# Rounding and absolute value of the first two chunks' angles on VectorE, clearing of the AT tiles on GpSimd, and another list of the order, in a gated linear attention with a low-rank mixer

## The chip, the cores and the metric

The kernel runs on one core of a Trainium2 chip. A core has five engines that each work through their own stream of instructions in order: TensorE (PE in the profile, with PEld for its loads of weights), VectorE (DVE), ScalarE (ACT), GpSimd (POOL) and SyncE (SP), which here only issues DMA transfers. They wait for one another by semaphores. The metric is the time of one execution on the device, in microseconds (us), and the number compared is the median of the runs.

## The reference, cut to what matters

Inputs are float32 for the attention (B = 4 batches, H = 8 heads, S = 768 tokens, D = 48 values a head); the weights of the mixer come in float64.

```python
mag = sqrt(a_re**2 + a_im**2)
scale = minimum(mag, 0.999) / (mag + 1e-6)
ar, ai = a_re * scale, a_im * scale          # a complex gate for each token, head and value
for t in range(S):                           # a complex state of 48 x 48 for each head
    S_re, S_im = ar*S_re - ai*S_im + k v^T, ar*S_im + ai*S_re
    y[t] = q S_re
x = y as (B, S, 384)
u = x + (x^T @ U @ V)^T                      # U: 768 x 32, V: 32 x 768, over the tokens
out = u + maximum(u @ w_ch1, 0) @ w_ch2      # 384 -> 1536 -> 384
```

The loop over tokens isn't run as such. Each batch is cut into chunks of 128 tokens. Within a chunk the product of the gates up to a token is exp(sum of log magnitudes) times a rotation by the sum of angles. So the queries and keys are scaled by exp(±sum) and by cosine and sine of the summed angle, and one matrix product gives all pairs of tokens. Sums over the tokens are matmuls with a triangular matrix of ones ("prefix"). A state of 96 x 48 for each head goes from chunk to chunk.

## The kernel before, in words

**Work.** There are 24 chunks i of 128 tokens (i = 0 to 23, six in a batch), taken in pairs, the groups g = 0 to 11. For group 0 each of its two chunks is treated by itself from the first step on; later groups are treated as pairs. The functions are:

- `magnitudes_of` and `ratio_of` (L674 to L731): squares, logarithms and exponentials on ACT and the sums between them on DVE give the logarithm of the clipped magnitude. The check of the smallest sums stands at L689, the first combination of squares at L686 (chunks of group 0), L715 begins the same for later groups, and L723 and L726 are its later sums.
- `within(i)`: L751 is PE's prefix sum into a bank of PSUM, and L754 are two Exps on ACT, with both signs, into `es`.
- `totals`: the last row of `es` goes out to DRAM (L762) and comes back spread over partitions as T (L765); L767 keeps its minimum on DVE.
- `turns_of` and `angles(i)` (L774 to L821): arctangent on ACT, then the prefix sum of the angles on PE (L811, and L814 by its caller, in whole turns; L817 carries in the last row of the chunk before). L819, on ACT, writes MAGIC − angle into F, which rounds to a whole number; L820, on DVE, takes MAGIC off again and adds the angle, so that F is the part of a turn that is left.
- `waves_of(i)` (L828 to L839): the absolute value of F (ACT, L837), the sine of F (L838) and the cosine, as a sine of the absolute value (L839), into `cs`.
- `prep(i)`: DVE multiplies queries and keys by `es` and by `cs` (L857 and L861, both by the helper `mul` in L462) into QKC; PE turns them (L872 to L874); ACT copies them from the banks into QK (L878).
- `chain(i)`: products of queries and keys (L901), their allowed part copied into an AT tile (L904), the state's product (L921 to L924), the state G after the first half chunk (GM, L932 or by a helper in L468) and after the second, times T (L462), and the outputs xo.
- `mixer(m)` from L976: the products with U, V, w_ch1 and w_ch2, which are most of PE's time. `single` (L587 to L618) makes float32 weights of float64 ones in integer steps, on DVE for the first six pieces.

Many lines of the profile are those of helpers: L459 is every ACT activation, L462 every DVE product, L465 every DVE sum, L468 a bounded sum.

**Buffers.** There are six banks of PSUM that most PE results share in turn, three QKC tiles, two AT tiles, and two F, `es` and `cs` buffers. The two AT tiles are cleared once, at L553 to L555, since L904 writes only the allowed places.

**Order.** Nothing runs while the functions are called: each registers operations by `PE(...)`, `ACT(...)`, `DVE(...)`, `POOL(...)` and `SP(...)`, with an engine, a cost, a rank and the data that it reads and writes, and each gets a number (2207 in all). Then the operations are issued in the order of a list, `ORDER`, written out by hand as numbers. What stands on one engine runs in the list's order; between engines only the data count. Two more things belong to the list: `SPARE` sets idle matmuls ahead of some operations (2 ahead of 122, 10 ahead of 132, 14 ahead of 193 and 5 ahead of 217), and `WARM` registers 7 and 5 more of them as operations 2205 and 2206. Their numbers are fixed; they are issued whether PE waits or not.

The operations that the change touches by number: 106 and 107 are the last two ACT steps (logarithm and Exp) that make x of chunk 0; 110 and 111 are chunk 0's two Exps of L754, 123 and 124 those of chunk 1; 122 is chunk 1's L751 pass, and 130 the load of ACT's next table. 133 and 138 are L819 for chunks 0 and 1, 134 and 139 their L820, 140 and 143 their L837, 141 and 144 their L838, and 142 and 145 their L839. 10 and 13 are steps of a weight piece on DVE, 191 is chunk 0's product of queries and keys with `es`, 192 and 196 are its two QKC products, and 151 is L715 of the next group.

Of the kernel before, what the change touches and what calls it, by code (L numbers as in the profile page):

```python
# [318 lines left out]
def kernel(  # L319
# [49 lines left out]
    RATIO, TINY = 1, 2.0 ** -60  # L369

    WARM = (7, 5)
    AT_ONCE = (0, 1, 2)
    WP = 768

    fast = ExitStack()
# [45 lines left out]
    def c_act(n):  # L421
        return 0.22 + 0.0008 * n
# [1285 lines left out]
```

## Time and profile before

| what | value |
|---|---|
| median of 3 runs | 535.88 us (535.63 to 535.94) |
| the profiled execution | 535.69 us |
| its span, first to last instruction | 533.9 us |
| mean granted TensorE clock | 0.998 |
| PE busy | 514.2 us, 96% of the span, 7494 instructions |
| DVE busy | 438.2 us, 82%, 863 instructions |
| ACT busy | 295.8 us, 55%, 531 instructions |
| POOL busy | 30.5 us, 6%, 58 instructions |
| read from memory and written | 33.60 MB and 4.76 MB |

The profile is one execution of the program as the hardware profiler saw it. Its times begin at the first instruction. In a row of a timeline the first number is the start, the second the duration (of all the instructions of the row, where it says x2 or more), then come engine, line, operation, the tiles out<-in, partitions x elements, and in brackets how long the engine was idle just before and what ended it. In a row of the waits the numbers are us in total, times, and the longest. Busy PE counts matmuls whose ends are modelled; register, branch and semaphore instructions aren't counted as busy.

### The profile page before, as it was taken

The numbers are of one execution on the slowest core, as the hardware profiler recorded it, in microseconds if no ns is written. First come the engines' busy times: TensorE is split into PE (matmuls) and PEld (weight loads), VectorE is DVE, ScalarE is ACT, GpSimd is POOL, SyncE is SP. The second block draws the span as 40 slices with busy tenths as digits, with TensorE's granted clock in tenths as the row PEclk, the third lists the DMA queues.
The fourth block names the chain that finished last, engine by engine and source line by source line (L and its number), as shares of the span: only waits on it lengthen the run. The fifth ranks groups of instructions, "written<-read, shape, count | busy, mean of one in ns | idle before, by whom it ended". The sixth has DMA issues, their size and how long they took to land.

```text
span 533.9 us, 17164 instructions
## 1 busy us (share of the span) xinstructions
PE 514.2 (96%) x7494; PEld 468.1 (88%) x7494; DVE 438.2 (82%) x863; ACT 295.8 (55%) x531; POOL 30.5 (6%) x58
## 2 busy tenths in 40 slices
PE   2899999999999999999999999999999999999996
PEld 1777786757989989999999999999999999999996
DVE  7898988999999998897886887786878866877842
ACT  5889998893776866546647655543555412221000
POOL 1000000001020001001100001100010000000010
PEclk9999999999999999999999999999999999999999
DMA  9967985565233423601534150500240000000002
GB/s 226 206 114 194 191 145 163 171 107 112 41 75 92 63 46 80 111 1 29 118 53 83 33 106 25 98 9 23 47 70 26 2 2 1 1 2 1 1 28 97
DMA packets 150706, 39.95 MB, mean 75 GB/s; under 512 B 145880, under 2 KB 147440, under 8 KB 150624
## 3 DMA queue, kind: packets, MB, share of 16 engines
q1 hardware_dynamic: 148544, 34.63, 32.3%
q0 software_dynamic: 2080, 4.15, 2.3%
q8 instruction: 61, 1.00, 0.8%
q14 instruction: 21, 0.17, 0.1%
HBM read 33.60 MB, written 4.76 MB: 72 GB/s over the span
## 4 chain that ended last, share of the span: by engine, by line
PE 81%; DVE 11%; ACT 3%; issue 2%; DMA 2%; SPq 0%; DVEq 0%; ACTq 0%
PE down L1313 20%; PE few L1181 13%; PE bank L1181 12%; PE bank L1484 7%; PE bank L872 4%; PE bank L901 4%; PE up L1074 3%; PE bank L959 3%; PE bank L921 3%; PE bank L951 2%; DVE QKC L462 2%; PE bank L1036 1%; PE bank L747 1%; PE bank L751 1%; PE bank L811 1%
## 5 line engine op out<-in xcount | busy, mean ns | idle before, releaser
L878 ACT COPY QK<-bank 112x512 f32<-112x512 f32 x96 | 51.8, 591 | 18.2 <-PE bank L872 17.9
L1313 PE MATMUL down<-w,h 128*128 128x192 f32 x288 | 53.6, 331 | 0.0
L462 DVE TENSOR_TENSOR QKC<-qk,cs 128x768 f32<-128x768 f32 x48 | 45.0, 951 | 4.9 <-ACT cs L459 4.7
L459 ACT ACTIVATE gate<-gate 128x768 f32<-128x768 f32 (+1 forms) x50 | 39.8, 798 | 16.3 <-DVE wide L719 12.7
L1313 PEld LDWEIGHTS down<-w,h 128*128 128x128 f32 x288 | 47.0, 190 | 0.9
L465 DVE TENSOR_TENSOR xo<-bank,xo 128x192 f32<-128x192 f32 x78 | 25.3, 350 | 24.9 <-PE bank L1484 16.0
L1189 ACT COPY h<-few 128x512 f32<-128x512 f32 x35 | 20.3, 585 | 30.0 <-PE few L1181 29.9
L1074 PE MATMUL up<-uT,w 128*128 128x256 f32 x144 | 34.0, 385 | 0.2
L456 ACT ACT_TABLE_LOAD x24 | 30.8, 1283 | 1.1 <-PEq L1692 0.7
L1074 PEld LDWEIGHTS up<-uT,w 128*128 128x128 f32 x144 | 26.6, 190 | 5.0 <-DVE xo L465 0.5
L1181 PE MATMUL bank<-extra,w 128*128 128x128 f32 x232 | 30.3, 276 | 0.0
L872 PE MATMUL bank<-ident,QKC 64*112 64x64 f32 x768 | 29.1, 221 | 1.0 <-DVE G L468 0.4
L872 PEld LDWEIGHTS bank<-ident,QKC 64*112 64x112 f32 x768 | 24.4, 130 | 6.2 <-DVE QKC L462 1.4
L459 ACT ACTIVATE es<-bank 128x384 f32<-128x384 f32 x48 | 20.3, 495 | 16.6 <-PE bank L747 15.8
L797 POOL DMA_DIRECT2D gate<-F x15 | 12.5, 832 | 285.2 <-DVE F L820 167.2
L1181 PEld LDWEIGHTS bank<-extra,w 128*128 128x128 f32 x232 | 28.3, 192 | 0.1
L1313 PE MATMUL down<-stage 128*128 128x192 f32 x144 | 28.0, 332 | 0.2 <-DVE xo L465 0.2
L465 DVE TENSOR_TENSOR xo<-down,xo 128x192 f32<-128x192 f32 (+1 forms) x58 | 22.0, 386 | 7.1 <-PE down L1313 6.9
L901 PE MATMUL bank<-QK 112*64 112x64 f32 x768 | 26.6, 224 | 0.0
L901 PEld LDWEIGHTS bank<-QK 112*64 112x64 f32 x768 | 24.2, 138 | 1.3 <-issue 0.5
L459 ACT ACTIVATE cs<-F 128x384 f32<-128x384 f32 x48 | 23.3, 516 | 3.0 <-DVE F L820 2.9
L1313 PEld LDWEIGHTS down<-stage 128*128 128x128 f32 x144 | 23.5, 190 | 1.2 <-DVE xo L465 0.5
(249 smaller groups left out, 1228.6 us busy)
## 6 DMA issues: line engine op xcount, KB each, us to landing
stage<-in_moe_w_ch_dram SPq DMA_DIRECT2D x12, 768.0 KB
gate<-in_a_re_dram SPq DMA_DIRECT2D x24, 192.0 KB
gate<-in_a_im_dram SPq DMA_DIRECT2D x24, 192.0 KB
qk<-in_q_dram SPq DMA_DIRECT2D x24, 192.0 KB
qk<-in_k_dram SPq DMA_DIRECT2D x24, 192.0 KB
VP<-in_v_dram SPq DMA_DIRECT2D x24, 192.0 KB
out_dram<-xo POOLq DMA_DIRECT2D x13, 192.0 KB, 2.9
out_dram<-xo POOLq DMA_DIRECT2D x16, 96.0 KB, 2.5
```

The costliest lines, as they stand in the source:

```text
L456: ACT(1.4, rank, lambda: nc.scalar.preload_act_table_set(name), writes=[TABLE])
L459: return nc.scalar.activation(out=o, in_=i, func=f, **kw)
L462: nc.vector.tensor_tensor(out=o, in0=a, in1=b, op=OP.mult)
L465: nc.vector.tensor_tensor(out=o, in0=a, in1=b, op=OP.add)
L872: nc.tensor.transpose(out=get(*ps[r])[0:DQ, h], in_=get(*qkc)[at, h].rearrange("p u d -> p (u d)")[:, 0:DQ], identity=ident[at, at], tile_ ...
L878: nc.scalar.copy(out=get(*QK)[0:DQ, u].rearrange("p (h t) -> p h t", t=CH)[:, :, r * HC:(r + 1) * HC], in_=get(*ps[r])[0:DQ])
L901: nc.tensor.matmul(out=get(*ps0)[r:r + HC, h], lhsT=k_of(h, r, HC), rhs=q_of(h, r, HC), start=True, stop=True, tile_position=(0, r))
L1074: nc.tensor.matmul(out=get(*ps)[:, e], lhsT=w1[:, f, (ff + e) * 128:(ff + e + 1) * 128], rhs=get(*uT)[:, f], start=(f == 0), stop=(f == KD ...
L1181: nc.tensor.matmul(out=get(*ps)[:, q], lhsT=w()[:, q * 128:(q + 1) * 128], rhs=v[0](), start=(n == 0 and q == 0), stop=True, skip_group_ch ...
L1189: ACT(c_act(n3 * CH) - 0.045, RU, lambda i=i, k=k: nc.scalar.copy(out=at(i, k), in_=get(*ps)), [ps], [o])
L1313: nc.tensor.matmul(out=get(*to)[:, part], lhsT=x(j), rhs=y[:, j], start=(first and j == 0), stop=(j == KH - 1), skip_group_check=not first)
L1484: nc.tensor.matmul(out=get(*ps), lhsT=w[0]()[:, q], rhs=x[0]()[:, q], start=(n == 0 and q == 0), stop=(q == k3 - 1), skip_group_check=True)
```

## The change

Three places in the code change, and the list.

```diff
-    AT_ONCE = (0, 1, 2)
+    AT_ONCE, ANGLES = (0, 1, 2), (0,)
...
         AT.append(singles.tile([128, H, HC], FP, name="AT%d" % n))
-        nc.vector.memset(AT[n], 0.0)
+        nc.gpsimd.memset(AT[n], 0.0)
...
+            if g in ANGLES:
+                DVE(c_one(DM) + 0.06, R2, lambda: nc.vector.tensor_scalar(out=fo(i), in0=get(*ps), scalar1=MAGIC, scalar2=MAGIC, op0=OP.add,
+                                                                          op1=OP.subtract), [ps], [f])
+                DVE(c_dve(DM), R2, lambda: nc.vector.tensor_tensor(out=fo(i), in0=get(*ps), in1=fo(i), op=OP.subtract), [ps], [f])
+                return
             ACT(c_act(DM), R2, lambda: act(fo(i), get(*ps), AF.Identity, scale=-1.0, bias=magic), [ps], [f])
...
-            ACT(ca, R2, lambda: act(half(0), ft(), AF.Abs), [f], [c0])
+            if g in ANGLES:
+                word = lambda a: a.bitcast(U32)
+                DVE(c_one(DM), R2, lambda: nc.vector.tensor_scalar(out=word(half(0)), in0=word(ft()), scalar1=0x7FFFFFFF, scalar2=None,
+                                                                   op0=OP.bitwise_and), [f], [c0])
+            else:
+                ACT(ca, R2, lambda: act(half(0), ft(), AF.Abs), [f], [c0])
```

For chunks 0 and 1 both steps of the rounding are now on DVE: the angle plus MAGIC minus MAGIC, from the bank, into F, and then the angle minus F. The absolute value is a bitwise step on DVE that clears the sign. The numbers of all operations stay the same; 133, 138, 140 and 143 go from ACT to DVE. The other 22 chunks keep the ACT steps.

The list differs from its position 29 to its position 1172 of 2207; what stands ahead and behind is the same. Its first lines, and the place of the T load:

```diff
-    ... 109, 110, 106, 121, 111, 107, 122,
-    123, 124, 130, 5, 4, 6, 9, 148, 11, 188, 8, 12, 15, 108, 14, 189, 149, 7, 131, 132, 135, 133, 147, 126, 212, 134, 140, 136, 137, 10, 191, 13, 146,
-    141, 142, 138, 139, 143, 144, 151, 145, 150, 152, 153, 213, 2, 125, 190, 192, 214, 128, 193, 196, 202, 203, 197, 215, 216, 220, 154, 155, 195,
-    204, 194, 156, 127, 199, 198, 17, 2205, 227, 205, 157, 206, 28, 158, 100, 2206, 221, 226, 228, 217, 18, 258, 229, 159, 160, 200, 161, 222, 19, 21,
+    ... 109, 110, 106, 121, 122, 123, 111,
+    107, 124, 130, 5, 4, 6, 9, 148, 188, 11, 8, 12, 15, 108, 14, 189, 149, 7, 131, 132, 135, 147, 126, 212, 133, 134, 136, 137, 10, 191, 140, 13, 146,
+    141, 142, 138, 139, 144, 143, 151, 145, 150, 152, 153, 213, 2, 125, 190, 192, 214, 128, 193, 196, 202, 197, 215, 216, 220, 154, 155, 195, 194,
+    156, 127, 199, 198, 17, 2205, 203, 204, 227, 205, 157, 206, 28, 158, 100, 2206, 221, 226, 228, 217, 18, 222, 258, 229, 159, 160, 200, 161, 19, 21,
...
```

By engine the moves are these:

- ACT: 123 stands ahead of 111 and 107 instead of behind them; 222 (a copy of chunk 1's turned keys into QK, L878) stands ahead of 159 (a logarithm of group 1, L725).
- DVE: 140 comes behind 191 and ahead of 13, and 143 behind 139; the stream is 133, 134, 10, 191, 140, 13, 138, 139, 143, 151, 192, 196. Further on some thirty steps trade places by a few positions: of the weight pieces (57, 81), of the mixer's sums (423, 424, 461, 464), of the copies into AT (714, 813) and of the magnitudes' sums (737, 836, both L723).
- PE: 203 (the second half of chunk 0's state product) comes behind 197 (turning chunk 0's keys) and the warm matmuls 2205, and with it 204, which waits for it on DVE (GM, L932); further on a dozen neighbours trade places (277 with 278, for example).
- SP: the load of chunk 0's queries (188) goes ahead of a piece of raw weights (11); the load of T for group 5 (751) goes ahead of a load of queries of chunk 12 (1209) and one of gates of chunk 15 (1163); 169, a load of T for group 1, ahead of a copy of V (25); two loads of raw weights (64, 70) move by a few positions.
- POOL: 440 (an output) and 1197 (a carry of angles, L797) move by a few positions.

155 rows, old and new, of the table ORDER are left out of this document.

## Prediction

> **What bounds the kernel now.** I read the page's fourth part (the chain that ended last), then busy time by stretches, then the waits of each engine, and only then the timelines of the first 35 us.
>
> ```profile
> PE 81%; DVE 11%; ACT 3%; issue 2%; DMA 2%; SPq 0%; DVEq 0%; ACTq 0%
> ```
>
> TensorE (PE) holds 81% of that chain. Next, busy time by stretches (length, then PE, PEld, DVE, ACT, POOL, granted clock, DMA share, GB/s).
>
> ```profile
> 0.00:29.50 29.50, 17.35 (x215) 14.02 (x215) 23.71 (x52) 20.27 (x35) 1.94 (x14) 1.00 0.96 210
> 29.50:250.00 220.50, 218.28 (x3438) 185.37 (x3439) 202.74 (x377) 165.48 (x289) 10.61 (x15) 1.00 0.49 102
> ```
>
> Up to 29.50 PE is idle for 29.50 − 17.35 = 12.15 us, and VectorE (DVE) is the busiest engine. From there to 250 us, over nearly all of the reordered stretch, PE is idle for only 220.50 − 218.28 = 2.22 us. So a delay at the start is kept to the end, and the moves behind it can return at most those 2.22 us. PE's work is the same in both kernels.
>
> The start on ScalarE (ACT) and PE; columns are start, duration, engine, line, what, and the idle time before it:
>
> ```profile
> 13.01 0.52 ACT L459 ACTIVATE gate<-gate 128x384 f32<-128x384 f32 x1
> 13.68 0.87 ACT L459 ACTIVATE es<-bank 128x384 f32<-128x384 f32 x2 [0.15 <-PE bank L751]
> 14.58 1.28 ACT L456 ACT_TABLE_LOAD   x1
> 17.60 0.58 ACT L459 ACTIVATE F<-bank,magic 128x384 f32<-128x384 f32 x1 [0.59 <-PE bank L814]
> 10.18 1.62 PE L751 MATMUL bank<-GL,prefix_r 128*128 128x384 f32 x2 [10.18 <-DVE GL L465]
> 12.44 1.20 PE L751 MATMUL bank<-GL,prefix_r 128*128 128x384 f32 x2
> 16.65 1.56 PE L814 MATMUL bank<-gate,prefix_z 128*128 128x384 f32 x4 [0.77 <-ACT gate L459]
> 18.82 0.91 PE L817 MATMUL bank<-F,ident 128*128 128x384 f32 x2 [0.61 <-DVE F L820]
> 29.55 0.66 PE L872 MATMUL bank<-ident,QKC 64*112 64x64 f32 x15 [0.43 <-DVE G L468]
> ```
>
> And DVE in the same stretch, with the few rows from which I take prices:
>
> ```profile
> 4.26 1.02 DVE L555 MEMSET AT<- 128x512 f32 x2
> 5.83 0.56 DVE L686 CUSTOM_DVE_ANT_0 GL<-gate 128x384 f32<-128x384 f32 x1
> 18.21 0.55 DVE L820 SCALAR_TENSOR_TENSOR F<-F,bank 128x384 f32<-128x384 f32 x1 [1.83 <-ACT F L459]
> 18.68 0.95 DVE L465 CUSTOM_DVE_ANT_0 w<-w,stage 128x1536 uint16<-128x1536 uint16 x1
> 19.55 0.95 DVE L462 TENSOR_TENSOR qk<-qk,es 128x768 f32<-128x768 f32 x1
> 20.91 0.54 DVE L820 SCALAR_TENSOR_TENSOR F<-F,bank 128x384 f32<-128x384 f32 x1
> 21.37 0.56 DVE L715 TENSOR_SCALAR GL<-gate 128x768 f32<-128x768 f32 x1
> 21.84 1.82 DVE L462 TENSOR_TENSOR QKC<-qk,cs 128x768 f32<-128x768 f32 x2
> 23.58 0.95 DVE L462 TENSOR_TENSOR qk<-qk,es 128x768 f32<-128x768 f32 x1
> 24.63 1.83 DVE L462 TENSOR_TENSOR QKC<-qk,cs 128x768 f32<-128x768 f32 x2
> 28.25 0.55 DVE L932 TENSOR_SCALAR GM<-bank 112x384 f32<-112x384 f32 x1
> 28.94 0.56 DVE L468 CUSTOM_DVE_ANT_0 G<-bank,GM 112x384 f32<-112x384 f32 x1
> 36.02 0.35 DVE L617 TENSOR_SCALAR UV<-UV 128x384 uint32<-128x384 uint32 x1
> ```
>
> From 18.21 to 29.5 DVE runs one instruction behind the other, and PE's first wait past 29.5 (0.43 us at 29.55) is for DVE's G at 28.94. Hence in this stretch an instruction more on DVE is paid in full, while ACT, which loses work there, waits for others. Neighbours overlap a little: 18.68 to 19.55 is a slot of 0.87 for a duration of 0.95. So an independent instruction costs its duration less 0.08. One that needs the result just before it starts later: 24.63 is 0.10 behind the end of 23.58 (+0.95), and 28.94 is 0.14 behind that of 28.25. I take 0.05 where both are simple.
>
> **The change, part by part.**
>
> (A) Clearing the AT tiles leaves DVE: 1.02 us at 4.26. The next link (5.83) waits for ACT's squares of gates that a DMA delivers:
>
> ```profile
> 4.95 0.84 ACT L459 ACTIVATE gate<-gate 128x768 f32<-128x768 f32 x1 [2.93 <-DMA gate<-in_a_im_dram]
> 1.30 0.80 POOL L539 MEMSET QKC<- 128x256 f32 x3
> 7.26 0.29 POOL L562 CAST prefix_r<-prefix_z 128x128 fp32r<-128x128 f32 x1 [5.01 <-DMA prefix_z<-in_spans_dram]
> ```
>
> The squares end at 4.95 + 0.84 = 5.79 whatever DVE does. GpSimd has 5.01 us of idle time ahead of the cast; a tile of 128x512 is twice the 128x256 that takes 0.80/3 = 0.27, so two of them cost about 1.1. **0.** Without that cover the cast would be late by at most the 1.1.
>
> (B) The order of the Exps on ACT. Chunk 1's first Exp now stands ahead of the second Exp of chunk 0 and the Exp of x (the row at 13.01). It can't start before 13.68, since it waits for the L751 pass that ends at 12.44 + 1.20 = 13.64. Two instructions that filled the time before now come behind it. Two such instructions take 0.87 in the row at 13.68, with the overlap of neighbours about 0.80. So the table load goes from 14.58 to 15.38, and all angles with it: the L814 pass, the first F, the whole DVE stretch. **+0.80** (0.4 if only one of the two falls behind, 0.85 with whole slots).
>
> (C) Rounding of chunk 0. Before: ACT at 17.60, 0.58, then DVE at 18.21, which is 0.61 later. After: DVE rounds from the bank. L932, a tensor-scalar operation out of a bank, takes 0.55; with 0.05 the subtraction starts 0.60 later. DVE is idle for 1.83 us there. **0** (−0.2 to +0.1, by the hop that goes and the wait that comes).
>
> (D) What is added to the gapless DVE stretch, ahead of the QKC products of chunk 0:
> - the absolute value of chunk 0, between two independent instructions. No row shows this operation. The nearest is L617, a bitwise step on 128x384 uint32 at 0.35; L715 does twice the elements in 0.56. The output is strided (every other block of 48), which no row shows for such a step. The other end is 0.55, as from a bank. I take 0.35, the row it is nearest to: 0.27 as a slot.
> - the rounding of chunk 1: 0.55 + 0.05 = 0.60. Nothing hides it now; on ACT such a step (0.58 at 17.60) lay beside DVE work.
> - its subtraction was followed by something independent (20.91 to 21.37, 0.46); now the absolute value needs it, 0.54 + 0.05: +0.13.
> - the absolute value of chunk 1: 0.27.
>
> Sum 0.27 + 0.60 + 0.13 + 0.27 = **+1.27** (0.97 with no penalties, 1.75 with both absolute values at 0.55 and the gaps of 0.10 to 0.14).
>
> Do the inputs come in time? With B the first F's bank is ready at 18.37, its subtraction ends at about 19.5, PE's carry pass (18.82 + 0.80, 0.91) at 20.5, and DVE rounds chunk 1 only at about 22.0. The cosine of chunk 0 is done at about 22.2 and that of chunk 1 at 24.4; DVE wants them at 23.91 and 26.7. So nothing else ends last. The first QKC pair moves from 21.84 to 21.84 + 0.80 + 1.27 = 23.91, and everything behind it on DVE and PE by the same **+2.07**: PE's filler matmuls are of fixed number and don't shrink, and the wait at 29.55 moves along.
>
> [...] No row of before shows this strided write.
>
> (E) Behind 29.5: a copy of transposed heads into QK now stands ahead of ACT's logarithm of the next group, which is then late by about half of a pair of copies.
>
> ```profile
> 29.11 1.06 ACT L878 COPY QK<-bank 112x512 f32<-112x512 f32 x2
> 31.36 0.84 ACT L459 ACTIVATE gate<-gate 128x768 f32<-128x768 f32 x1
> 32.39 0.95 DVE L726 SCALAR_TENSOR_TENSOR GL<-GL,gate 128x768 f32<-128x768 f32 x1
> 33.63 1.56 PE L751 MATMUL bank<-GL,prefix_r 128*128 128x384 f32 x4
> ```
>
> One copy of a pair of 1.06 is about 0.5. The logarithm ends at 31.36 + 0.84 = 32.20, 0.19 ahead of L726, whose end at 33.34 is 0.29 ahead of PE's L751 pass at 33.63. So 0.5 − 0.19 − 0.29 leaves 0.02; I take **+0.05** (0 to 0.3, if the second slack isn't one).
>
> (F) The other moves, to position 1172 of the list. The load of T for group 5 goes ahead of three loads on SP's queue. By the chain its DMA ends at 183.18 + 4.58 = 187.76 and DVE waits for it:
>
> ```profile
> 183.18 4.58 DMA T<-TD
> DVE G L462 <- DVE G L468: 0.7, 1, 0.7
> DVE GL L723 <- ACT gate L459: 1.0, 1, 1.0
> DVE h L1193 <- PE few L1181: 1.0, 1, 1.0
> DVE h L465 <- PE few L1181: 0.7, 1, 0.7
> PE bank L747 <- DVE GS L738: 0.6, 1, 0.6
> PE bank L747 <- DVE extra L1115: 0.5, 1, 0.5
> PE down L1313 <- DVE xo L465: 0.2, 1, 0.2
> ```
>
> DVE loses 0.7 us there, but the only wait of PE that can follow from it is the 0.2 of L1313; no wait of PE of that size stands beside it. The moved w1 pieces, loads and sums belong to waits of DVE of 0.7 to 1.0, which PE doesn't see. PE's waits for GS and extra (0.6, 0.5) may shrink or grow. I take **−0.3**: the 0.2 and a little of the others (−2.2, all of PE's idle time, to +0.3).
>
> Sum: 0 + 0.80 + 0 + 1.27 + 0.05 − 0.3 = **+1.8 us**. The profiled run took 535.69 us, of which 533.9 is its span and 1.8 lies around it; the median of the runs is 535.88. So the profiled run would be 537.5, and the median 535.88 + 1.8 = **537.7**. A measurement of this kernel can tell about 0.2%, or 1.07 us, from no change; +1.8 is beyond it. With the bounds of B to E the forecast's own range is 537.0 to 538.6.
>
> **Rivals.**
>
> *The new order gives it back* (no change that can be told). From 29.5 on PE could catch up with what it now waits for, if the moved instructions end its waits for GS and extra, the 0.43 and the 0.2. That is up to 1.73, say 1.4 where I take 0.3: 535.88 + 2.1 − 1.4 = 536.6. Or B is wrong by half, which gives 536.4 with the smaller returns. For: PE has those four waits and no others of note. Against: all of them would have to go. It decides from 1.0 us returned.
>
> *DVE is the real bound behind 29.5* (faster). If DVE's waits count in full, the order that removes the four shown (0.7 + 1.0 + 1.0 + 0.7 = 3.4) would bring 2.1 − 3.4 = −1.3: 534.6. For: those waits lie in the reordered stretch, and the T load is plainly moved ahead. Against: PE is busy for 218.28 of 220.50 us there, so 3.4 can't come out of 2.22; it would need more than PE's idle time. It decides from 3.2 us returned.
>
> *The clock falls in the longer gaps* (slower). PE's gap before 16.65 grows from 0.77 to about 1.6 us, and one of about 1.2 opens ahead of the first transposes. The first passes at 10.18 took 1.62 for two; later ones of that form took 0.91 (18.82). If the array fell back to that rate for twice the 1.62 us that the row shows, 3.2 us, it would lose 0.71/1.62 of them: +1.4, so 537.7 + 1.4 = 539.1. For: the rows show that both rates occur. Against: the gap of 0.77 left 1.56 for four at 16.65. [...] The trace has no gap between 0.77 and 10.18 to show it.
>
> *Dearer pieces* (slower): both absolute values at 0.55 with all penalties and no return from F: 535.88 + 0.80 + 1.75 + 0.05 + 0.3 = 538.8.
>
> **How the numbers follow.** Forecast (537.7) 0.62; the order gives it back (about 536.5) 0.17; DVE is the bound (534.6) 0.07; the clock (539.1) 0.07; dearer pieces (538.8) 0.07. That makes slower by over 0.2% 0.62 + 0.07 + 0.07 = 0.76, within 0.2% 0.17, faster 0.07. The range 535.9 to 539.2 takes in all but the DVE case and the outer ends of the others.
>
> **What would show it.** Right: the table load at about 15.4 and the first F product's end at about 18.4 (B); DVE without gaps from its first rounding to about 31.5, with two absolute values of 0.35 and two roundings of 0.55 (C, D); the first QKC pair's end at about 25.65 instead of 23.58; PE's last short wait at about 31.6; PE idle for about 2 us from 31.5 to 252. Wrong: a first QKC pair that isn't late, which would void B or D; or PE idle for under 1 us behind it, which would mean that F returned more than I give it.

## The result and the profile after

The changed kernel takes 538.42 us (median of 4 runs, 538.26 to 539.14) where the kernel before took 535.75 (4 runs, 535.20 to 535.94): +2.67 us, a ratio of 1.0049 with a 95% interval of 1.0037 to 1.0061. It is slower, by half a per cent. The forecast was 537.7 in a range of 535.9 to 539.2. The profiled execution took 538.26 us with a span of 536.5, against 535.69 and 533.9.

The chain that ended last, and then busy time by stretches (length, then PE, PEld, DVE, ACT, POOL, granted clock, DMA share, GB/s), first of the changed kernel, then of the kernel before. Both are cut at the same work: at the end of TensorE's wait for G (31.92 and 29.55), and at a block of L1190 products (L1181 before) with which the reordered stretch is over:

```profile
PE 82%; DVE 13%; ACT 2%; issue 2%; DMA 1%; SPq 0%; DVEq 0%; ACTq 0%
```

```profile
0.00:31.92 31.92, 18.20 (x216) 14.73 (x216) 24.80 (x54) 18.55 (x31) 2.86 (x16) 1.00 0.92 198
31.92:249.19 217.27, 215.37 (x3405) 181.99 (x3406) 201.52 (x373) 161.37 (x283) 10.49 (x15) 1.00 0.49 102
```

```profile
29.55:246.41 216.86, 214.69 (x3406) 181.78 (x3406) 200.93 (x373) 161.85 (x283) 10.61 (x15) 1.00 0.49 103
```

TensorE is idle for 31.92 − 18.20 = 13.72 us of the start, where it was 29.55 − 17.35 = 12.20, and some of what it does there takes longer. Behind that it is idle for 217.27 − 215.37 = 1.90 us, where it was 216.86 − 214.69 = 2.17: the later moves have made it idle for 0.27 less. But the same matmuls keep it busy for 215.37 − 214.69 = 0.68 longer, so the reordered stretch takes 0.41 more, not less.

The start on ScalarE, VectorE, GpSimd and TensorE (start, duration, what):

```profile
14.02 0.87 ACT L458 ACTIVATE es<-bank 128x384 f32<-128x384 f32 x2 [1.30 <-PE bank L750]
14.78 0.53 ACT L458 ACTIVATE gate<-gate 128x384 f32<-128x384 f32 x1
15.19 0.49 ACT L458 ACTIVATE es<-bank 128x384 f32<-128x384 f32 x1
15.70 1.28 ACT L455 ACT_TABLE_LOAD   x1
```

```profile
2.19 0.98 POOL L554 MEMSET AT<- 128x512 f32 x2
```

```profile
5.81 0.56 DVE L685 CUSTOM_DVE_ANT_0 GL<-gate 128x384 f32<-128x384 f32 x1 [0.23 <-ACT gate L458]
...
18.72 0.56 DVE L819 TENSOR_SCALAR F<-bank 128x384 f32<-128x384 f32 x1 [1.56 <-PE bank L813]
19.31 0.56 DVE L821 TENSOR_TENSOR F<-bank,F 128x384 f32<-128x384 f32 x1
...
21.52 0.35 DVE L843 TENSOR_SCALAR cs<-F 128x384 uint32<-128x384 uint32 x1
...
22.29 0.55 DVE L819 TENSOR_SCALAR F<-bank 128x384 f32<-128x384 f32 x1
22.87 0.56 DVE L821 TENSOR_TENSOR F<-bank,F 128x384 f32<-128x384 f32 x1
23.46 0.36 DVE L843 TENSOR_SCALAR cs<-F 128x384 uint32<-128x384 uint32 x1
...
24.20 1.82 DVE L461 TENSOR_TENSOR QKC<-qk,cs 128x768 f32<-128x768 f32 x2
...
31.30 0.56 DVE L467 CUSTOM_DVE_ANT_0 G<-bank,GM 112x384 f32<-112x384 f32 x1
```

```profile
12.43 1.55 PE L750 MATMUL bank<-GL,prefix_r 128*128 128x384 f32 x2
...
17.77 1.56 PE L813 MATMUL bank<-gate,prefix_z 128*128 128x384 f32 x4 [1.02 <-ACT gate L458]
...
25.21 0.66 PE L881 MATMUL bank<-ident,QKC 64*112 64x64 f32 x16 [1.25 <-DVE QKC L461]
...
31.92 0.66 PE L881 MATMUL bank<-ident,QKC 64*112 64x64 f32 x15 [0.44 <-DVE G L467]
...
35.99 1.56 PE L750 MATMUL bank<-GL,prefix_r 128*128 128x384 f32 x4
```

Read them against the rows of before. The table load has gone from 14.58 to 15.70, by 1.12. The first QKC pair has gone from 21.84 to 24.20, by 2.36. G on VectorE (31.30 for 28.94), TensorE's wait for it (31.92 for 29.55) and the next prefix pass (35.99 for 33.63) are all later by the same 2.36 or 2.37. Between the first rounding and G, VectorE has no gap that counts (it is busy for 12.20 of the 12.58 us from 18.72 to 31.30). So 2.36 of the 536.5 − 533.9 = 2.6 us between the two profiles has come into being by 24 us: 1.12 on ScalarE ahead of the table load, and 2.36 − 1.12 = 1.24 on VectorE behind it.

### The profile page after: what moved, and what is told of

Same layout as the page of the kernel before. It is cut to its first block, busy times and chain, and to the rows that moved or that the text cites. A ratio compares the mean times of both kernels' runs of the same rounds, so it can differ in the third digit from the quotient of the medians.

```text
span 536.5 us, 17164 instructions
## 1 busy us (share of the span) xinstructions
PE 515.8 (96%) x7494; PEld 469.1 (87%) x7494; DVE 439.7 (82%) x865; ACT 293.5 (55%) x527; POOL 31.3 (6%) x60
## 4 chain that ended last, share of the span: by engine, by line
PE 82%; DVE 13%; ACT 2%; issue 2%; DMA 1%; SPq 0%; DVEq 0%; ACTq 0%
PE down L1322 19%; PE few L1190 13%; PE bank L1190 12%; PE bank L1493 7%; PE up L1083 4%; PE bank L910 4%; PE bank L881 4%; PE bank L968 4%; PE bank L930 3%; PE bank L960 2%; DVE QKC L461 2%; PE bank L1045 1%; PE bank L750 1%; PE bank L810 1%; PE bank L746 1%
## 5 line engine op out<-in xcount | busy, mean ns | idle before, releaser
L1322 PE MATMUL down<-w,h 128*128 128x192 f32 x288 | 53.9, 331 | 0.0
L1322 PEld LDWEIGHTS down<-w,h 128*128 128x128 f32 x288 | 47.0, 190 | 1.0
L881 PE MATMUL bank<-ident,QKC 64*112 64x64 f32 x768 | 29.6, 221 | 2.3 <-DVE QKC L461 1.9
L881 PEld LDWEIGHTS bank<-ident,QKC 64*112 64x112 f32 x768 | 24.6, 130 | 8.0 <-DVE QKC L461 3.0
L1190 PE MATMUL bank<-extra,w 128*128 128x128 f32 x232 | 30.3, 276 | 0.0
L1190 PEld LDWEIGHTS bank<-extra,w 128*128 128x128 f32 x232 | 28.3, 192 | 0.1
L1322 PE MATMUL down<-stage 128*128 128x192 f32 x144 | 27.9, 332 | 0.0
L1322 PEld LDWEIGHTS down<-stage 128*128 128x128 f32 x144 | 23.5, 190 | 0.7
```

The source lines that it names most:

```text
L881: nc.tensor.transpose(out=get(*ps[r])[0:DQ, h], in_=get(*qkc)[at, h].rearrange("p u d -> p (u d)")[:, 0:DQ], identity=ident[at, at], tile_ ...
L1190: nc.tensor.matmul(out=get(*ps)[:, q], lhsT=w()[:, q * 128:(q + 1) * 128], rhs=v[0](), start=(n == 0 and q == 0), stop=True, skip_group_ch ...
L1322: nc.tensor.matmul(out=get(*to)[:, part], lhsT=x(j), rhs=y[:, j], start=(first and j == 0), stop=(j == KH - 1), skip_group_check=not first)
```

## The experiments

The theory of the start says: 0.8 us by the order of the Exps, 1.27 by the steps added to VectorE, all of it kept to the end, and about nothing by the later moves. Its rivals are that the list alone, or the later moves, make the loss; that the late end of the L750 pass makes it; and that the clock falls in the longer gaps. The numbers of the table are medians, with the interval of the ratio to the kernel before on the same chip.

| run | us | before | ratio (95%) |
|---|---|---|---|
| e1_list: new list, old code | 537.59 | 535.85 | 1.0028 (1.0017 to 1.0038) |
| e2_code: new code, old list | 537.12 | 535.85 | 1.0018 (1.0009 to 1.0027) |
| e3_exps: whole change, Exps as before | 538.08 | 535.85 | 1.0037 (1.0025 to 1.0050) |
| e4_later: later moves alone | 536.42 | 535.85 | 1.0008 (0.9999 to 1.0017) |
| e5_again: whole change | 538.78 | 535.56 | 1.0057 (1.0044 to 1.0071) |
| e6_clear: clearing alone | 535.90 | 535.56 | 1.0008 (0.9999 to 1.0017) |
| e7_abs: absolute values alone | 536.43 | 535.56 | 1.0014 (1.0005 to 1.0024) |
| e8_fill: weight steps into the gap | 535.20 | 535.56 | 0.9992 (0.9983 to 1.0001) |
| e9_warm: ten idle matmuls early | 537.39 | 535.79 | 1.0029 (1.0017 to 1.0042) |
| e10_both: e8 and e9 together | 536.73 | 535.79 | 1.0024 (1.0009 to 1.0039) |
| e11_start: whole change, later list of before | 537.61 | 535.79 | 1.0034 (1.0022 to 1.0046) |
| e12_whole: whole change | 538.71 | 535.79 | 1.0051 (1.0035 to 1.0068) |

**e1_list.** The file of the kernel before, with the list of the changed one.

```diff
 ORDER = (
-    91, 93, 95, ... 110, 106, 121, 111, 107, 122, 123, 124, ...
+    91, 93, 95, ... 110, 106, 121, 122, 123, 111, 107, 124, ...
```

> The kernel before with the new list alone: ACT keeps rounding and absolute value, VectorE keeps the clearing of AT. Theory of the start: only the order of the Exps costs, chunk 1's first Exp ahead of chunk 0's second Exp and the Exp of x: +0.80 us, table load at about 15.4 (15.7 if the array's clock opens as late as in the changed kernel's profile), the list behind it returns nothing: 536.5. Rival, the list gives something back behind the start: 535.9 or less. Rival, the later list itself costs: over 537.0.

It is 1.74 us slower, twice the 0.8. Its ScalarE rows show the Exps:

```profile
13.74 0.88 ACT L466 ACTIVATE es<-bank 128x384 f32<-128x384 f32 x2 [1.04 <-PE bank L758]
...
15.42 1.28 ACT L463 ACT_TABLE_LOAD   x1
```

From the first Exp of chunk 1 to the table load it is 15.42 − 13.74 = 1.68 us, where before it was 14.58 − 13.68 = 0.90: the order costs 0.78, as reckoned. The other 0.96 of the 1.74 is not at the start; it must come from the later moves, as the second rival has it, or from a spread of that size.

**e2_code.** The file of the changed kernel, with the list of before, so that the absolute values stand right behind their subtractions.

```diff
 ORDER = (
-    ... 106, 121, 122, 123, 111, 107, 124, ... 147, 126, 212, 133, 134, 136, 137, 10, 191, 140, 13, ...
+    ... 106, 121, 111, 107, 122, 123, 124, ... 133, 147, 126, 212, 134, 140, 136, 137, 10, 191, 13, ...
```

> The changed code with the list of before. Theory of the start: the gapless stretch of VectorE gets 0.27 + 0.60 + 0.13 + 0.27 (and no change by the Exps, so the table load stays at about 14.6, or 14.9 with a late clock): +1.3 us, 537.0; the first pair of QKC products starts about 1.3 us later than in the kernel before, at about 23.1. Rival, VectorE has slack there and the loss of the change came from its list: within 0.3 us of the kernel before.

+1.27 us, the number of the forecast. On ScalarE and VectorE:

```profile
14.77 1.28 ACT L463 ACT_TABLE_LOAD   x1
```

```profile
23.39 1.82 DVE L469 TENSOR_TENSOR QKC<-qk,cs 128x768 f32<-128x768 f32 x2
```

The pair is 23.39 − 21.84 = 1.55 later, of which 14.77 − 14.58 = 0.19 was there at the table load: 1.36 on VectorE. The rival that VectorE has slack there is out. In this kernel both absolute values stand right behind their subtractions, so by the forecast's own prices it should lose 0.27 + 0.60 + 0.13 + 0.27 + 0.13 = 1.40; the rows' 1.36 bears that out, and that the time shows the very number of the forecast is luck.

**e3_exps.** The changed kernel with 123 moved back behind 107.

```diff
-    ... 106, 121, 122, 123, 111, 107, 124, ...
+    ... 106, 121, 122, 111, 107, 123, 124, ...
```

> The changed kernel whole, but chunk 1's first Exp is back behind chunk 0's second Exp and the Exp of x. Theory of the start: it is 0.80 us faster than the changed kernel, so 1.9 us behind the kernel before, 537.6; table load at about 14.6 to 14.9. Rival, the late end of the L750 pass (1.55 us instead of 1.20) and not the order of the two Exps made ScalarE late: then only some 0.1 to 0.3 us is won, 538.2.

The second L750 pass took 1.55 us here too, as in the changed kernel, and the table load is 15.70 − 14.85 = 0.85 earlier all the same:

```profile
14.85 1.28 ACT L463 ACT_TABLE_LOAD   x1
```

So the order of the two Exps is worth 0.8 us at the table load, and the late pass some 0.3 beside it. The time alone doesn't decide: +2.23 over the kernel before, where the whole change had +2.67, +3.22 and +2.92 in its three measurements, none of them beside this one. That is 0.44 to 0.99 faster, and the median of 538.08 lies nearer to the rival's 538.2 than to the 537.6 that was expected.

**e4_later.** The kernel before, new list from position 122 on.

```diff
-ORDER = before
+ORDER = before[:122] + after[122:]
```

> The kernel before with its own list up to position 121, and the new list from there on (all moves behind about 33 us, the T load among them). Theory of the start: no change beyond 0.3 us either way, 535.5 to 536.0, since TensorE has only 2.2 us of idle time there and the moves end few of its waits. Rival, the moves give back over 1 us: 534.7 or less. Rival, they cost: 536.5 or more.

+0.57 us, with an interval that just takes in zero. The moves certainly don't give back over 1 us; more likely they cost.

**e5_again.** The changed kernel unchanged, on the next chip.

> The changed kernel once more, beside the other parts on one chip. Theory of the start (Exps 0.8, VectorE 1.3, nothing behind): 2.1 us over the kernel before plus what its later list costs (0 to 0.6 by the kernel with the later moves alone), 538.0 to 538.6. The second L750 pass takes anything between 1.20 and 1.55 us if its length is the clock's phase and not the change; 1.55 again would speak for the change.

+3.22 us, and again a second L750 pass of 1.55.

**e6_clear.** The kernel before with one line of the change.

```diff
-        nc.vector.memset(AT[n], 0.0)
+        nc.gpsimd.memset(AT[n], 0.0)
```

> The kernel before with only the clearing of the AT tiles on GpSimd. Forecast's term A: nothing, within 0.3 us of the kernel before; the first combination of squares (L686) still starts at 5.8. Rival, VectorE's early second of freedom moves the start: 0.2 us or more faster, with L686 earlier.

+0.34, a little over the 0.3 that was allowed, with an interval that reaches from nothing to 0.9. L686 starts at 5.87, L685 of the changed kernel at 5.81, and that of before at 5.83. The bracket of the changed kernel's row above shows why: VectorE is free earlier, and then waits 0.23 us for ScalarE's squares. By the rows A is nothing at the start; the time alone doesn't rule out a small cost.

**e7_abs.** Rounding and clearing as before (the first of the two conditions, in `angles`, is off); only the two absolute values on VectorE, list of before.

```diff
-            if g in ANGLES:
+            if False:
...
-        nc.gpsimd.memset(AT[n], 0.0)
+        nc.vector.memset(AT[n], 0.0)
```

> The kernel before with only the two absolute values on VectorE, each right behind its subtraction, rounding and clearing where they were, list of before. Theory of the start: two times 0.27 and two times 0.13 for the wait on the instruction just before: +0.80 us, 536.65, and the first QKC pair as much later. Rival, ScalarE's relief (two steps of about 0.4 less) brings the second rounding earlier and VectorE has room: 0.3 or less. Rival, the strided absolute value runs at 0.55: +1.2.

+0.87 us for the 0.80 that was expected. The rows show the absolute value at its price, and the pair 1.17 later, with the table load 0.37 later on its own account (14.95 for 14.58, by the late pass): 0.80.

```profile
19.18 0.36 DVE L851 TENSOR_SCALAR cs<-F 128x384 uint32<-128x384 uint32 x1
...
22.26 0.36 DVE L851 TENSOR_SCALAR cs<-F 128x384 uint32<-128x384 uint32 x1
...
23.01 1.82 DVE L469 TENSOR_TENSOR QKC<-qk,cs 128x768 f32<-128x768 f32 x2
```

```profile
14.95 1.28 ACT L463 ACT_TABLE_LOAD   x1
```

The rounding is then 1.36 − 0.80 = 0.56 of e2's 1.36; the forecast had 0.60.

**e8_fill.** The other way round: roundings on VectorE, absolute values on ScalarE, clearing on GpSimd, list of before, but two weight steps moved out of the stretch into VectorE's idle time ahead of the first rounding, and two idle matmuls fewer ahead of 193.

```diff
-    ... 132, 135, 133, 147, 126, 212, 134, 140, 136, 137, 10, 191, 13, 146, ...
+    ... 132, 135, 10, 13, 133, 147, 126, 212, 134, 140, 136, 137, 191, 146, ...
-    122: 2, 132: 10, 193: 14, 217: 5,
+    122: 2, 132: 10, 193: 12, 217: 5,
```

> The kernel before with both roundings on VectorE but the absolute values on ScalarE, the clearing on GpSimd, and two steps of weight pieces (10, 13; 0.87 and 0.52 us) moved ahead of the first rounding into VectorE's idle 1.83 us; two idle matmuls fewer ahead of 193. Theory of the start (VectorE sets the pace from 18.2 to 29.5, what leaves that stretch is gained): the first QKC pair starts at about 21.5 instead of 21.84, 0.3 us faster than the kernel before, 535.5. Rival, ScalarE or the carry pass on TensorE is late next: no change, and the added 0.6 of rounding shows: 536.4.

```profile
21.57 1.82 DVE L469 TENSOR_TENSOR QKC<-qk,cs 128x768 f32<-128x768 f32 x2
```

The pair starts at 21.57, 0.27 ahead of before although the second pass was late here too (its table load came at 14.86, 0.28 late). The time is 535.20 for 535.56: −0.36, with an interval that just takes in no change. The mechanism holds, the gain is no more than likely. It is the only one of the twelve whose median is below the kernel before; none is shown to be faster.

**e9_warm and e10_both.** Ten idle matmuls ahead of operation 109, in the kernel before and in e8.

```diff
-    122: 2, 132: 10, 193: 14, 217: 5,
+    109: 10, 122: 2, 132: 10, 193: 14, 217: 5,
```

> The kernel before with ten idle matmuls more, ahead of chunk 0's L751 pass (operation 109), where TensorE has been idle since the start. If the length of the second L751 pass (1.20 to 1.55 us so far) is the clock's phase, the array is now warm: the first pass takes about 0.9 instead of 1.62, the second about 0.9, and the Exps of chunk 1 start at about 13.45 instead of 13.7 to 14.0. All behind moves by that: 0.2 to 0.5 us faster, 535.3. Rival, the idle 1 to 2 us between the last idle matmul and the pass close the clock again (the forecast's clock rival): passes of 1.62 and 1.2 to 1.55 as before, no change.

> The kernel with both roundings on VectorE and the weight steps in its idle time, and the ten idle matmuls as well. By the theory of the start the two gains add: 0.3 to 0.5 from the first and 0.2 to 0.5 from the second, 534.8, first QKC pair at about 21.2. Rival, an earlier table load meets the weight steps, which end only at 17.8, and the second gain is lost: 535.2.

Both came out slower instead of faster: +1.60 and +0.94. Of e9_warm, TensorE's rows, its waits, and two stretches:

```profile
1.55 3.99 PE L1636 MATMUL bank<-ident 128*128 128x128 f32 x20 [1.55 <-DVE bank L386]
10.15 1.62 PE L751 MATMUL bank<-GL,prefix_r 128*128 128x384 f32 x2 [4.61 <-DVE GL L465]
...
12.41 1.55 PE L751 MATMUL bank<-GL,prefix_r 128*128 128x384 f32 x2
```

```profile
PE bank L921 <- issue: 2.1, 2, 1.1
```

```profile
9.00:10.10 1.10, 0.00 (x0) 0.00 (x0) 1.00 (x5) 0.52 (x1) 0.00 (x0) 0.50 1.15 352
12.40:14.00 1.60, 1.60 (x6) 0.99 (x5) 1.57 (x4) 1.09 (x3) 0.00 (x0) 0.50 0.84 126
```

The idle matmuls ran out at 5.54, much sooner than I had reckoned, and left a gap of 4.61 us. The granted clock, 1.00 up to 7.5 us, fell to 0.50 in it and was still there at 14, and the passes took 1.62 and 1.55, no less than without the idle matmuls. The second pass is 1.20 us long in the profile of before, 1.26 in e11_start, 1.33 in e2_code and 1.55 in the changed kernel, although they begin alike. That the clock makes its length was my guess, and no run here shows it: the granted clock reads 1.00 over the whole start in the profile of before, the first pass of 1.62 among it, and in that of the changed kernel, whose second pass took 1.55. The long second pass puts e9_warm's first QKC pair 0.31 back (22.15 for 21.84), which is far from 1.6. What goes with the rest of the loss is 2.1 us in two waits that the profile puts down to issue, where before has none of over 0.3 us; e10_both has 1.0 and 0.5, although its first QKC pair starts at 21.44, 0.40 ahead of before. Which resource these waits are for the trace doesn't say, and no run shows that they are what makes the kernels slower. It stays open.

**e11_start and e12_whole.** The changed kernel with the list of before from position 122 on, and the changed kernel whole, on one chip.

```diff
-ORDER = after
+ORDER = after[:122] + before[122:]
```

> The changed code with the new list up to position 121 and the list of before from there on: the changed start without the later moves. By the theory of the start 0.8 + 1.3 over the kernel before, 537.7; if the later moves cost what the kernel with them alone showed, it is some 0.3 to 0.6 us faster than the changed kernel beside it; if they cost nothing, equal to it.

> The changed kernel, beside the one with its start alone. By the earlier runs 2.7 to 3.2 us over the kernel before, 538.3 to 538.8. Second L750 pass between 1.20 and 1.55 if its length is the clock's phase.

+1.82 and +2.92: the start alone costs about what A to D say (2.07), and the later list costs another 1.10. Together with e4_later's 0.57, and the 0.96 left over in e1_list, three pairs point the same way. In the last pair every run of e12_whole (538.21 to 539.31) took longer than every run of e11_start (537.34 to 538.13), on the same chip.

Where is it? Again by stretches that are cut at the same work, from the first pass of four prefix matmuls (L758 in the one, L750 in the other) to the block of products behind the reordered stretch, of e11_start and then of e12_whole:

```profile
36.48:248.81 212.33, 210.38 (x3303) 178.08 (x3301) 197.00 (x365) 157.66 (x276) 10.61 (x15) 1.00 0.49 103
```

```profile
36.13:249.38 213.25, 211.33 (x3304) 178.28 (x3301) 197.81 (x366) 157.66 (x276) 10.51 (x15) 1.00 0.49 103
```

The stretch is 0.92 longer, and all of that is busy time: TensorE is busy for 211.33 − 210.38 = 0.95 more over the same matmuls, and idle for 1.92 instead of 1.95. One place can be read off directly. In e6_clear, with the list of before, and in e12_whole TensorE does the same transposes (L872, now L881) and products (L1313, now L1322):

```profile
230.76 1.11 PE L872 MATMUL bank<-ident,QKC 64*112 64x64 f32 x32
231.80 1.24 PE L1313 MATMUL down<-stage,h 128*128 128x192 f32 x6
232.88 0.81 PE L1313 MATMUL down<-stage 128*128 128x192 f32 x4
```

```profile
233.70 0.66 PE L881 MATMUL bank<-ident,QKC 64*112 64x64 f32 x16
234.29 1.24 PE L1322 MATMUL down<-stage,h 128*128 128x192 f32 x6
235.46 0.66 PE L881 MATMUL bank<-ident,QKC 64*112 64x64 f32 x16
236.05 1.24 PE L1322 MATMUL down<-stage 128*128 128x192 f32 x6
```

The list of before has both blocks of transposes together (x32), the new one has a product between them. To the start of the last product it is 232.88 − 230.76 = 2.12 us before and 236.05 − 233.70 = 2.35 after, 0.23 more for two more changes between kinds of matmul, with no wait in the profile. And TensorE's waits behind 33 us, of e6_clear and then of e12_whole, have changed places rather than gone:

```profile
PE bank L747 <- DVE GS L738: 0.6, 1, 0.6
PE bank L747 <- DVE extra L1115: 0.5, 1, 0.5
PE bank L872 <- DVE QKC L462: 0.4, 1, 0.4
```

```profile
PE bank L881 <- DVE QKC L461: 0.6, 2, 0.4
PE bank L746 <- DVE extra L1124: 0.5, 1, 0.5
PE rank L1004 <- ACT xo L978: 0.5, 1, 0.5
...
PE down L1279 <- ACT h L458: 0.2, 1, 0.2
```

GS's 0.6 went; 0.5 for xo, 0.2 more for QKC and 0.2 for h came. With the shorter waits that these rows leave out they even out, as the idle time of 1.92 for 1.95 shows.

## Why the prediction was right, and where not

- **A, the clearing: 0.** Right. GpSimd cleared both tiles in 0.98 us (1.1 was reckoned) from 2.19, far ahead of its next work, and L685 didn't move.
- **B, the Exps: +0.80.** Right: 0.78 by e1_list's rows. The other 0.34 of the 1.12 at the table load is the second L750 pass, 1.55 us instead of 1.20. It is not the change's doing: e4_later, with the old start, has its table load at 14.90, and e3_exps, with the old order of the Exps, at 14.85. The profile of before happens to have the shortest second pass of all, so the forecast's rows began 0.3 early.

```profile
14.90 1.28 ACT L463 ACT_TABLE_LOAD   x1
```

- **C, chunk 0's rounding: 0.** Right: 19.31 − 18.72 = 0.59 from the start of the rounding to that of the subtraction, 18.21 − 17.60 = 0.61 before.
- **D, VectorE's gapless stretch: +1.27.** Right: 1.24 in the changed kernel, and 1.36 for the code alone, where 1.40 was due. The absolute values took 0.35 and 0.36 with their strided output, the price of the L617 row, so the 0.55 end of the bound is out. The second rounding took 0.55 and the subtraction behind it started 0.58 later (0.60 was reckoned).
- **E, the copy ahead of the logarithm: +0.05.** Nothing, if anything: the prefix pass at 35.99 is 2.36 behind the one of before, as the whole stretch is.
- **F, the other moves: −0.3.** This step failed, by its sign. The forecast had it that "PE's waits for GS and extra (0.6, 0.5) may shrink or grow" and took the 0.2 of L1313 and a little more as a return. The T load did what it should on VectorE, where G times T now starts right behind G:

```profile
189.51 0.56 DVE L467 CUSTOM_DVE_ANT_0 G<-bank,GM 112x384 f32<-112x384 f32 x1
190.11 0.56 DVE L461 TENSOR_TENSOR G<-G,T 112x384 f32<-112x384 f32 x1
```

  0.60 from one to the other where it was 188.41 − 187.19 = 1.22, in the rows of before:

```profile
187.19 0.55 DVE L468 CUSTOM_DVE_ANT_0 G<-bank,GM 112x384 f32<-112x384 f32 x1
188.41 0.56 DVE L462 TENSOR_TENSOR G<-G,T 112x384 f32<-112x384 f32 x1 [0.66 <-DVE G L468]
```

  TensorE had little from it: with the later list its idle time was 0.03 us less in e12_whole than in e11_start, and 0.27 less in the changed kernel than in before. In place of a return there was a cost, 0.57 us in e4_later and 1.10 between e11_start and e12_whole. The cost is busy time, 0.95 and 0.68 us more in the same two pairs. I had reckoned with idle time alone, and took "PE's work" to be "the same in both kernels" because its matmuls are; in another order the same matmuls kept TensorE busy for longer. Changes between kinds of matmul are seen to cost 0.23 us at one place; that they make the rest as well is not shown.

The sum was 1.8 and came out at 2.67: B and D make 2.07, and F makes up the rest with about +0.6 instead of −0.3. (The two profiles divide it otherwise, 2.36 by 24 us and 0.41 behind, since 0.34 of the 2.36 is the long second pass.) That the result lies within the forecast's own range of 537.0 to 538.6 is in part luck: the range gave F no room at all, and the widths of B and D took up an error that was not theirs. (With C at its −0.2 its low end would be 536.8, not 537.0.) The signs that the forecast named came, each about 0.3 late, by the long second pass: the table load at 15.70 for 15.4, the end of the first QKC pair's work, where the next product starts, at 25.94 for 25.65, and TensorE's last short wait of the start at 31.92 for 31.6.

Of the rivals, *the new order gives it back* is out by e4_later and e11_start. *DVE is the real bound behind 29.5* is out: VectorE's wait for T went, and nothing came of it. *The clock falls in the longer gaps* is out: the gaps grew to 1.02 and 1.25 us (17.77 and 25.21), the four L813 matmuls behind the first still took 1.56, as before, and the granted clock reads 1.00 up to 31.92. *Dearer pieces* named nearly the right total (538.8) mostly for the wrong reason: its absolute values at 0.55 weren't there. But it speaks of no return from F, and its sum has a cost of 0.3 in that place, which is nearer to what F did.

## What to carry to other kernels

Look for the stretch where the bound engine waits for another one that has no gap: here the steps that were moved onto that other engine were paid in full (1.24 us where 1.27 was reckoned), although VectorE's share of the whole span of before was 82%, and what they relieved (ScalarE, busy for only 6.68 of the 12.58 us from the first rounding to G) gave nothing. Before moving an instruction ahead of others on an in-order engine, ask what it waits for: an Exp that couldn't start before 13.7 us made late the two that could have filled the time before it, and the table load behind them by 0.78. And with an engine that is 99% busy, don't look at its waits alone: the same work in another order kept TensorE busy for 0.95 us longer in e12_whole than in e11_start, and at one place two more changes between kinds of it went with 0.23.

## What the runs showed that I had not expected

Ten idle matmuls on an idle TensorE made the kernel 1.6 us slower; two waits put down to issue go with that, and what they wait for is open. The later order made TensorE's same matmuls 0.95 us longer without a wait showing; at one place two more changes of kind went with 0.23 us, from which I estimate about 0.1 each. And the second L750 pass is anything from 1.20 to 1.55 us long from one profile to the next, which alone moves the start by up to a third of a microsecond: a profile of one execution can be that lucky.
